# Half of x by crossbar DMA, query norms on GpSimd, two VectorE shifts in one instruction, in a gated mix of attention and MLP

## The chip, the cores and the metric

The kernel runs on one core of a Trainium2 chip. The metric is the device time of one execution in microseconds, as the median of several executions. A profiled execution has a span as well, which is 1.7 to 2.1 us shorter than its time; where stretches of one execution are compared, they are stretches of spans. The granted clock is the share of full speed at which TensorE's clock was let run; it is given where it differs.

## The reference, cut to what matters

```python
# x [1, 2048, 512]; wqkv [512, 1536]; wo [512, 512]; w_gate, w_up [512, 1792]; w_down [1792, 512]; gate_w [512]
g = sigmoid((x * gate_w).sum(-1, keepdims=True))
q, k, v = split(x @ wqkv)                      # 32 heads of 16
p = softmax(q @ k.T * 16 ** -0.5)              # 32 x 2048 x 2048 scores
a = (p @ v) @ wo
b = (sigmoid(x @ w_gate) * (x @ w_up)) @ w_down
out = g * a + (1 - g) * b                      # all in bfloat16
```

The scores are the bulk: 2048 blocks of 128 keys by 512 queries, each of which has to go through an exponential.

## The kernel before: the parts that matter

The work is cut into 32 units of 512 queries by 4 heads, 64 score blocks each. A block's exponential is taken in one of two ways. ScalarE takes two or three blocks in one Exp instruction. VectorE takes one block with an integer trick: a linear function of the score, written as a 16-bit integer whose bits are then read as a float16 (`make_x`), and two shifted copies of a pair of blocks (three phases that are averaged by three products P.V in place of one). The table `D_HALVES` says how many pairs of blocks ("halves") of each unit go to VectorE:

```python
D_PAIR = ((2, 0), (3, 1))
D_HALVES = (8, 8, 8, 8, 9, 6, 10, 8, ...)          # 32 entries, sum 267
...
def make_exp(ts):                                   # two or three blocks, ScalarE
    ... a.activation(some(PA, out), some(ps_all, bs), ACTF.Exp, bias=ACT_BIAS, scale=SCALE)
def make_x(ds):                                     # one block, VectorE
    ... v.tensor_scalar(PDu[:, bp.slot, 0, i:i + len(ds), :], some(ps_all, bs), EXP_A, EXP_B, op0=ALU.mult, op1=ALU.add)
...
for m in range(1, NPH):                             # two shifts per half
    x = P.add("dve", 0.36, lambda v, bp=bp, m=m: v.tensor_scalar(
        PDu[:, bp.slot, m, :, :], PDu[:, bp.slot, 0, :, :], float(PH_OFF[m]), None, op0=ALU.add), ...)
```

Nothing is issued in this textual order. The program holds a list scheduler: each instruction is added as a task with a planned duration, a simulation of the five engines picks an order by priorities (some forty tuned constants, many with a value per unit), and that order is then written out as five fixed instruction streams with semaphores. So the order on every engine is static, and the planned durations decide it. DMA is planned so, with one lane for all transfers:

```python
if t.dma:
    begin = max(self.dma_free, now + 2.5)
    self.dma_free = begin + t.nbytes / 330e3
    vis = self.dma_free + 0.6
```

x is loaded in plain layout and turned by TensorE, with copies out of PSUM (the memory that TensorE's products go to, `ps_all` in the lines) on VectorE and ScalarE. A query's norm is a square on GpSimd, a product with a constant matrix on TensorE and an addition on VectorE. Attention outputs are turned by DMA from SBUF to SBUF, and the MLP's output weights (`w_down`, 1.75 MB) are loaded in the middle of the run, near 158 us.

## Time and profile before

| | value |
|---|---|
| time, median of 3 (range) | 755.96 us (755.88 to 756.47) |
| profiled span, granted clock | 754.4 us, 0.999 |
| first exp starts, last exp ends | 19.9, 743.1 us |
| ScalarE idle between those two | 0.9 us |
| blocks on ScalarE, on VectorE | 1514, 534 |

The lines themselves are in the prediction below. They are read in the order busy shares, chain of waits, groups, stretches.

For the comparison I use one more measure, which needs no further lines: the length of a unit from its first exp to the first exp of the next unit. The exps run in a fixed order, and the scheduler is plain Python, so its order names the units of each exp and the trace gives the exp's start. An exp can hold blocks of two units, so one boundary can be read up to one exp (0.9 us) either way.

### The profile page before, as it was taken

The page shows a single profiled execution, that of the slowest core. Times are in us where ns is not written, and L with a number is a line of the kernel's source. Part 1 is how long each engine was busy: PE and PEld are TensorE (multiplying, and loading weights), DVE is VectorE, ACT ScalarE, POOL GpSimd, SP SyncE. Part 2 cuts the span into 40 slices and gives each one's busy share as a digit, 9 for nine tenths or more (in the row PEclk, how much of TensorE's full clock was granted, in tenths as well). Part 3 has the DMA queues.
Part 4 walks back from the last instruction along what each step waited for, and adds up shares of the span by engine and source line. Part 5 has one row for each costly group of instructions (what it writes and reads, how often), then busy time and mean ns, then how long its engine had stood idle before and what let it go on. Part 6 is the DMA issues. An engine that isn't in the chain of part 4 may idle for free.

```text
span 754.4 us, 21827 instructions
## 1 busy us (share of the span) xinstructions
PE 739.0 (98%) x9617; PEld 218.0 (29%) x9617; DVE 663.1 (88%) x1311; ACT 734.7 (97%) x822; POOL 111.4 (15%) x198
## 2 busy tenths in 40 slices
PE   8999999999999999999999999999999999999997
PEld 5233232332222222222222222222222222222222
DVE  4999999999898988778899888998889888978986
ACT  5999999999999999999999999999999999999994
POOL 4532625420100101001010010101001000000000
PEclk9999999999999999999999999999999999999999
DMA  9300000040000000000010000000000010000000
GB/s 299 121 10 9 16 4 16 9 115 9 8 9 9 16 16 22 23 2 16 9 17 9 9 23 17 22 9 17 9 1 16 16 23 23 9 10 8 15 2 30
DMA packets 34839, 19.22 MB, mean 25 GB/s; under 512 B 26688, under 2 KB 32696, under 8 KB 34744
## 3 DMA queue, kind: packets, MB, share of 16 engines
q1 hardware_dynamic: 33352, 16.38, 8.4%
q8 instruction: 75, 1.23, 0.7%
q10 hardware_dynamic: 1392, 1.44, 0.6%
q14 instruction: 20, 0.16, 0.1%
HBM read 9.70 MB, written 2.10 MB: 16 GB/s over the span
## 4 chain that ended last, share of the span: by engine, by line
ACT 75%; PE 19%; DVE 4%; DMA 1%; ACTq 0%; issue 0%; DVEq 0%
ACT PA L920 72%; PE ps_all L746 7%; PE ps_all L946 6%; PE ps_all L955 5%; ACT tT L904 3%; DVE PD L928 1%; DVE PD L984 1%; DMA PD<-in_A_x_dram 1%; PE ps_all L749 1%; PE ps_all L866 0%; DVE un L779 0%; DVE am L792 0%; PE ps_all L729 0%; DVE ost L1077 0%; ACTq L635 0%; DVE Q L830 0%
## 5 line engine op out<-in xcount | busy, mean ns | idle before, releaser
L920 ACT ACTIVATE PA<-ps_all 128x1024 bf16<-128x1024 f32 (+1 forms) x744 | 710.5, 1177 | 0.9 <-PE ps_all L946 0.5
L928 DVE TENSOR_SCALAR PD<-ps_all 128x512 uint16<-128x512 f32 x534 | 357.2, 685 | 59.8 <-PE ps_all L946 43.4
L946 PE MATMUL ps_all<-Q,K 32*128 32x512 bf16 x2048 | 301.5, 384 | 6.1 <-ACT PA L920 4.6
L955 PE MATMUL ps_all<-PA,V 128*17 128x512 bf16 x1514 | 242.3, 382 | 1.0 <-ACT PA L920 0.7
L984 DVE TENSOR_SCALAR PD<-PD 128x1024 uint16<-128x1024 uint16 x534 | 216.9, 438 | 4.2
L955 PE MATMUL ps_all<-PD,Vm 128*17 128x512 f16 x1068 | 189.9, 381 | 0.2 <-DVE PD L984 0.2
L946 PEld LDWEIGHTS ps_all<-Q,K 32*128 32x128 bf16 x2048 | 75.0, 91 | 303.5 <-ACT PA L920 272.5
L955 PE MATMUL ps_all<-PD,V 128*17 128x512 f16 x534 | 146.3, 382 | 0.0
L746 PE MATMUL ps_all<-xT,wg 128*32 128x512 bf16 x896 | 74.5, 384 | 0.0
L955 PEld LDWEIGHTS ps_all<-PA,V 128*17 128x17 bf16 x1514 | 55.9, 88 | 55.5 <-issue 43.2
L746 PE MATMUL ps_all<-un,hT 128*32 128x512 bf16 x896 | 71.7, 383 | 0.0
L746 PE MATMUL ps_all<-xT,wu 128*32 128x512 bf16 x896 | 70.0, 383 | 0.1
L1022 POOL TENSOR_TENSOR rs<-rec,e 128x16 f32<-128x16 f32 x32 | 8.3, 259 | 407.3 <-DVE rec L1020 407.3
L955 PEld LDWEIGHTS ps_all<-PD,Vm 128*17 128x17 bf16 x1068 | 44.2, 88 | 34.3 <-issue 26.2
L907 DVE SCALAR_TENSOR_TENSOR hT<-tT,ps_all 128x512 bf16<-128x512 bf16 x56 | 38.1, 680 | 8.6 <-PE ps_all L746 7.6
L904 ACT ACTIVATE tT<-ps_all 128x512 bf16<-128x512 f32 x56 | 42.7, 762 | 0.0
L831 POOL TENSOR_TENSOR qsq<-Q 128x512 bf16<-128x512 bf16 x15 | 16.0, 1069 | 159.7 <-DVE Q L830 159.7
L955 PEld LDWEIGHTS ps_all<-PD,V 128*17 128x17 bf16 x534 | 33.6, 88 | 18.5 <-issue 14.9
L784 POOL TENSOR_SCALAR K<-un,msk 128x512 bf16<-128x512 bf16 x28 | 26.6, 954 | 8.6 <-DVE un L771 5.8
L746 PEld LDWEIGHTS ps_all<-xT,wu 128*32 128x32 bf16 x896 | 19.7, 95 | 26.2 <-issue 13.6
L746 PEld LDWEIGHTS ps_all<-xT,wg 128*32 128x32 bf16 x896 | 17.8, 94 | 26.1 <-issue 20.4
L746 PEld LDWEIGHTS ps_all<-un,hT 128*32 128x32 bf16 x896 | 17.6, 94 | 24.3 <-issue 19.0
(92 smaller groups left out, 331.6 us busy)
## 6 DMA issues: line engine op xcount, KB each, us to landing
wg<-in_B_w_gate_dram SPq DMA_DIRECT2D x1, 1792.0 KB, 11.0
wu<-in_B_w_up_dram SPq DMA_DIRECT2D x1, 1792.0 KB, 14.4
un<-in_B_w_down_dram SPq DMA_DIRECT2D x1, 1792.0 KB, 8.2
out_dram<-ost SPq DMA_DIRECT2D x14, 128.0 KB, 1.8
PD<-in_A_x_dram SPq DMA_DIRECT2D x4, 256.0 KB, 5.6
PD<-in_A_x_dram ACTq DMA_DIRECT2D x4, 256.0 KB, 6.8
un<-in_A_wqkv_dram SPq DMA_DIRECT2D x2, 384.0 KB, 8.8
mid<-mid SPq DMA_TRANSPOSE x45, 2.4
```

Of the source, the lines that this page charges most:

```text
L746: i = pe.matmul(bk(b)[32 * j:32 * j + 32, :], w()[:, 32 * j:32 * j + 32], x(), start=first, stop=last, tile_position=(0, 32 * j), skip_gro ...
L749: return (MM, lambda pe: pe.matmul(bk(b), w(), x(), start=first, stop=last), four)
L784: eK[g, r, c] = P.add("pool", 1.0, lambda p, r=r: p.tensor_scalar(K[:, g, r, c * 512:(c + 1) * 512], kraw[:, kr.slot, :], msk[:, r:r + 1], ...
L831: s = P.add("pool", 1.15, lambda p: p.tensor_tensor(qsq[:, sq.slot, :], Q[:, bq.slot, 0, :], Q[:, bq.slot, 0, :], ALU.mult), [ev], [sq, bq ...
L904: et = P.add("act", 0.48, lambda a: a.activation(tT[:, t_.slot, :], bk(b), ACTF.Tanh, scale=0.5), [l1], [b, t_], kind="m")
L907: e_h[c, ft] = P.add("dve", 0.62, lambda v: v.scalar_tensor_tensor(hT[:, h_.slot, :], tT[:, t_.slot, :], 1.0, bk(b2), ALU.add, ALU.mult), ...
L920: e = P.add("act", 0.175 + 0.3665 * len(ts), lambda a: a.activation(some(PA, out), some(ps_all, bs), ACTF.Exp, bias=ACT_BIAS, scale=SCALE) ...
L928: return P.add("dve", 0.076 + 0.534 * len(ds), lambda v: v.tensor_scalar(PDu[:, bp.slot, 0, i:i + len(ds), :], some(ps_all, bs), EXP_A, EX ...
L946: return pe.matmul(bk(b), K[32 * j:32 * j + 32, g, r, kt * 128:(kt + 1) * 128], Q[32 * j:32 * j + 32, bq.slot, r, :], start=True, stop=Tru ...
L955: return pe.matmul(bk(bpv)[32 * j:32 * j + DH + 1, :], lhs(h), rhs(), start=t.first, stop=t.last, tile_position=(0, 32 * j), skip_group_ch ...
L984: x = P.add("dve", 0.36, lambda v, bp=bp, m=m: v.tensor_scalar(PDu[:, bp.slot, m, :, :], PDu[:, bp.slot, 0, :, :], float(PH_OFF[m]), None, ...
L1022: e2_ = P.add("pool", 0.2, lambda p: p.tensor_tensor(r4(rs), r4(rec), e2[:, 4 * c:4 * c + 4][:, :, None].to_broadcast([128, 4, 4]), ALU.mu ...
```

## The change

The intent: move more exponentials off ScalarE (16 more halves), and pay for it by taking other work off VectorE and TensorE: query norms by DMA and GpSimd, two shifts in one instruction, half of x turned (transposed) by the DMA crossbar on the way in. The rest is a new tuning of the scheduler. Its core, abridged, with `...` for what is cut:

```diff
-D_PAIR = ((2, 0), (3, 1))
-D_HALVES = (8, 8, 8, 8, 9, 6, 10, ...)      # sum 267
+D_PAIR = ((3, 2), (1, 0))
+D_HALVES = (9, 9, 8, 8, 10, 6, 10, ...)     # sum 283
+X_TURN, X_LOAD = (0, 1), (2, 3)
-FIN, FIN_STEP, LAST, LAST_STEP = (12.0, 18.53, 25.2), ...
+FIN, FIN_STEP, LAST, LAST_STEP = (12.33, 18.53, 24.22), ...
 ...                                          # all other constants retuned
@@ scheduler
-            begin = max(self.dma_free, now + 2.5)
-            self.dma_free = begin + t.nbytes / 330e3
-            vis = self.dma_free + 0.6
+            q = t.kind == "turn"
+            self.dma_free[q] = max(self.dma_free[q], now + (2.0 if q else 2.5)) + t.nbytes / (200e3 if q else 330e3)
+            vis = self.dma_free[q] + 0.6
 ...                                          # two ready shifts are merged; products of the next unit may go first
@@ x
+        if c in X_TURN:
+            eT[c] = [dma_t(lambda c=c: xT[:, :, 512 * c:512 * c + 512], lambda c=c: x_v[512 * c:512 * c + 512, :], ..., 524288, 60 - c, 2.1)]
@@ query norms
-    s = P.add("pool", 1.15, ... qsq = Q * Q)
-    l2 = P.group(key - 8.0, [full(b2, wn, qsq, True, True)], ...)          # TensorE
-    en = P.add("dve", 0.68, ... nsb = b2 + a_[:, g:g + 1])
+    s, d, e, _ = head_sums(lambda: Q[:, bq.slot, 0, :], [ev], [bq])        # DMA turn, GpSimd square, four halving sums
+    d2 = dma_t(lambda: mdt(s2), lambda: md(s), [e], [s, s2])
+    en = pl(0.95, ... md(s2) * -0.5 + a2[:, g:g + 1])
@@ shifts
+    def phase(x):
+        def emit(v):
+            at = sorted(b.slot for b in x.sets)                            # one or two halves
+            a = PDu[:, at[0]:at[-1] + 1:..., :, :, :]
+            return v.tensor_scalar(a[:, :, x.n, :], a[:, :, 0, :], float(PH_OFF[x.n]), None, op0=ALU.add)
-    N_PD = 3, N_MID = 11
+    N_PD = 4, N_MID = 10
 ...                                          # DMA semaphores shared, waits on the own engine kept
```

## The prediction

> **What bounds the kernel now.** I read the busy shares first, then the tenths, then the chain of waits, then the groups by form, and last three stretches of time.
>
> ```profile
> PE 739.0 (98%) x9617; PEld 218.0 (29%) x9617; DVE 663.1 (88%) x1311; ACT 734.7 (97%) x822; POOL 111.4 (15%) x198
> ACT 75%; PE 19%; DVE 4%; DMA 1%; ACTq 0%; issue 0%; DVEq 0%
> ```
>
> Three engines look full. The chain that ended last is ScalarE for three quarters; the rest is TensorE at the two ends of the span. Its pieces in order of time show what ScalarE's work costs when it follows itself:
>
> ```profile
> 2.28 7.03 DMA PD<-in_A_x_dram
> 19.98 2.31 ACT PA L920 x2
> 180.08 8.25 ACT PA L920 x9
> 188.33 0.49 ACT tT L904
> ```
>
> Nine exps over two score blocks each take 8.25 us, so 0.917 us each and 0.458 us a block (the 1164 ns below is one instruction from end to end; neighbours overlap). A tanh of the MLP takes 0.49. The groups by form:
>
> ```profile
> L920 ACT ACTIVATE PA<-ps_all 128x1024 bf16<-128x1024 f32 x718 | 677.9, 1164 | 0.5 <-PE ps_all L946 0.5
> L928 DVE TENSOR_SCALAR PD<-ps_all 128x512 uint16<-128x512 f32 x534 | 357.2, 685 | 59.8 <-PE ps_all L946 43.4 <-PE ps_all L955 13.5
> L984 DVE TENSOR_SCALAR PD<-PD 128x1024 uint16<-128x1024 uint16 x534 | 216.9, 438 | 4.2
> L920 ACT ACTIVATE PA<-ps_all 128x1536 bf16<-128x1536 f32 x26 | 39.2, 1518 | 0.4 <-PE ps_all L955 0.4
> L837 DVE TENSOR_SCALAR nsb<-ps_all,a_ 128x512 bf16<-128x512 f32 x15 | 10.9, 730 | 0.0
> L734 ACT ACTIVATE xT<-ps_all 128x1024 bf16<-128x1024 bf16 x4 | 4.1, 1024 | 3.3 <-PE ps_all L729 3.3
> ```
>
> ScalarE idles about 1 us before 744 exps. It turns 718 x 2 + 26 x 3 = 1514 of the 2048 score blocks into exps; VectorE does the other 534 by its integer trick (one read of PSUM each, and two shifts per pair of blocks). The sum closes: first exp at 19.9 us, 1514 x 0.458 = 693.4, 56 tanhs x 0.49 = 27.4, some 1.7 of small work and gaps, last exp ended at 743.1, then a tail of 11.3 to 754.4. So the middle is bound by ScalarE, to within a microsecond. VectorE and ScalarE by stretch:
>
> ```profile
> 20.00:60.00 40.00, 38.32 (x537) 12.15 (x536) 36.94 (x74) 39.80 (x44) 16.38 (x25) 1.00 0.14 50
> 60.00:150.00 90.00, 88.83 (x1343) 28.07 (x1338) 88.79 (x174) 90.00 (x98) 41.49 (x58) 1.00 0.05 11
> 300.00:500.00 200.00, 197.41 (x2437) 53.80 (x2429) 175.73 (x348) 200.00 (x227) 13.91 (x24) 1.00 0.07 15
> ```
>
> (PE, PEld, DVE, ACT, POOL in that order.) VectorE is full too until 150 us, and has 12% free from 300 to 500. TensorE's 98% is no measure, as its 384 ns records overlap. The chain shows 0.216 us a streamed matmul of 512 columns (ten in 2.16 us). In the last 20 us, where TensorE sets the pace, a set of scores with its switch into that mode takes 0.32 and two sets of others 0.55, so a switch either way costs about 0.11. My estimate of the work: some 735 score sets and 779 sets of four P.V products at 0.216; 960 full matmuls at 0.216 or their equal (projections, MLP, output, norms); and 735 x 2 x 0.11 for switches. That is 159 + 168 + 207 + 162 = 696 us in 735: TensorE has about 5% of slack. All three are near the edge, ScalarE is over it.
>
> **What the Trainium skill says.** "ScalarE: Activation LUTs", section "What ACT_TABLE_LOAD costs", gives an ACTIVATE 186 ns (280 with a pointer bias) plus 0.833 ns a column, back-to-back ones overlapping by about 93 ns. The trace has 1164 ns at 1024 columns but starts 917 apart, so an overlap of 247; I use the trace. "VectorE: DVE Perf Modes", section on the TRN2 errata, gives an SBUF to SBUF instruction 58 cycles plus a quarter of its columns in 4x mode: 325 ns for 1024 columns, 594 for 2048. The trace's closest pairs of shifts start 330 ns apart, which agrees; the fused size is not in this trace. "SBUF — State Buffer", section "Who interferes with whom", says that such VectorE instructions and GpSimd's exclude each other for a whole instruction. The trace agrees in direction. These are the shifts alone, busy time and count in the same stretches:
>
> ```profile
> 60.00:150.00 90.00, 30.41 (x68) 1.00 0.05 11
> 500.00:740.00 240.00, 69.43 (x177) 1.00 0.06 12
> ```
>
> 0.447 us where GpSimd is busy 46%, 0.392 where 5%. "DMA: Bandwidth & Descriptors", section "Latency and other measured facts", gives a crossbar transpose 261 GB/s with a non-contiguous middle dimension. This trace, in slices of 1 us from 440 on:
>
> ```profile
> DMA  6000000000000003070000000000000003000052
> GB/s 131 0 0 0 0 0 16 0 0 0 0 0 0 0 8 131 8 147 1 0 0 0 0 0 0 0 0 0 16 0 0 0 0 131 0 0 0 0 102 46
> ```
>
> The 128 KB stores (slices 16 and 34) took 0.3 of the engines' microsecond, the 128 KB transposes (slices 1 and 18) 0.6 to 0.7: about twice the DMA time a byte, near 200 GB/s. I use that.
>
> **The change, part by part.**
>
> 1. Blocks moved. The table of halves per unit sums to 283 instead of 267, so 566 blocks go to VectorE and 1482 to ScalarE. ScalarE loses 32 x 0.458 = 14.7 us on the binding path. VectorE gains 32 x 0.669 = 21.4 for the reads and 32 x 0.406 = 13.0 for the shifts (busy time over count in the groups above). TensorE gains two products per block, 64 or 16 sets of four, 3.5 us.
>
> 2. Query norms. Fifteen 0.73 us additions leave VectorE, -10.9 us, and fifteen matmuls TensorE, -3.2, with their PSUM banks. They become two transposes, a square, four halving sums and one scale-and-add per query. From the 1.05 us square and the 0.95 us masked copy in the trace I put GpSimd's extra at about 2.6 us a query, 40 in all: 111 to about 150 us. The latency of a query's norm grows from 6 us (43.5 to 50.2 for the first) to perhaps 13. Queries have four buffers and are made units ahead, so this is hidden. The cost is the lock: 0.055 us more per shift at 41 points more GpSimd, some 3.8 us per 37 us, so +4 us of VectorE for 40 more.
>
> 3. Fused shifts. Each fused pair saves one fixed cost, 0.06 us by the page and up to 0.09 by the trace's mean over its bare columns. At most 283 pairs exist; both must be ready together, which a full VectorE and a fourth buffer favour. I assume 150, -11 us. VectorE in all: 663.1 + 21.4 + 13.0 - 10.9 + 4 - 11 - 1.4 (two key copies moved to ScalarE) = 678, of a shorter span 92%. In the crowded stretch to 150 us it gets only three more halves (units 0, 1 and 4) and loses four or five norm additions: about level at 98%.
>
> 4. Start. Now x lands at 9.3, its last transpose is evacuated at 14.0, and the first exp follows 5.9 us later. Half of the 64 transposes (about 2.5 us of TensorE) and four 1.02 us ScalarE copies go. The DMA side gets dearer: 1 MB turned at 200 GB/s takes 5.2 us instead of the 3.1 at the plain rate. The last turned chunk would land near 11 to 11.5, but it is then usable at once. 11.5 + 5.9 gives 17.4; I take the first exp at 17.4, -2.5 us. ScalarE's two extra key copies (0.6 each) lie in idle time there.
>
> 5. Retuned order, a look into the next unit's products, waits on the own engine, shared DMA semaphores. I see no term of their own; they decide whether ScalarE stays fed.
>
> TensorE in all: 696 + 3.5 - 3.2 - 2.5, less 16 score sets and their switches (16 x 0.43 = 6.9): 687 of about 720. Its slack stays near 4 to 5%.
>
> Sum: span 754.4 - 14.7 - 2.5 = 737.2, plus new gaps in ScalarE that I guess at 2 us from three nearly full engines: 739.2. Timed runs lie 1.6 above the profiled span (755.96 against 754.4), so 740.8; the retuned tail may give a little back, so I say **740**.
>
> **The rivals.** (a) VectorE takes over as the bound: if few shifts fuse and the lock costs twice my figure, VectorE reaches 693 us and stays full to 150 us, and exps wait for banks there. For it: 98.7% from 60 to 150. Against: 12% free later, where most of the new halves lie. It gives 745 to 750. (b) TensorE becomes the bound, since products triple for each moved block; gaps of 5 to 8 us appear before exps. Against: the norms and score sets leave. It gives 744 to 748. (c) The crossbar feeds the start late: if turning 1 MB beside loads runs at half of 200 GB/s, the start gains nothing, 743. (d) The start gains 4 to 5 us, as evacuation and not landing set it, and the other timings leave ScalarE without gaps: 734 to 737.
>
> **Range and chances.** The 14.7 us are nearly certain, as they are counted; alone they are 1.94%. The 2% mark is 740.8 us, so the verdict hangs on the start's gain against new gaps. Range 732 to 747. Faster by over 2%: 0.55, as several freedoms (fusing, one more buffer, retuning) all point one way. Within 2%: 0.43. Slower: 0.02.
>
> **What would show it right or wrong.** Right: exps over 1482 blocks at 0.458 us, ScalarE still without idle, first exp near 17.4, VectorE near 678 with a group of 128x2048 shifts near 0.6 us, GpSimd near 150. Wrong: ScalarE idle of over 6 us released by TensorE's scores (b) or by VectorE (a); shifts over 0.5 us per 1024 columns (a); first exp after 19.5 (c); or a price per block other than 0.458, which would break the sum itself.

## The result, and the profile after

| | before | after |
|---|---|---|
| median (range) of 4 runs each, us | 755.92 (755.84 to 756.47) | 758.0 (756.42 to 759.62) |
| profiled span, us | 754.4 | 756.1 |
| first exp starts, us | 19.9 | 22.15 |
| ScalarE idle from first to last exp, us | 0.9 | 12.6 |
| ScalarE's work there, us | 722.3 | 709.2 |

The ratio is 1.0026 (95% interval 1.0004 to 1.0048): the same. Ratios here are the mean time of one kernel's fast runs over that of the other's in the same rounds, so not quite the ratio of the medians beside them. ScalarE lost 13.1 us of work and gained 11.7 of idle.

The page of the changed kernel: busy time by engine, the granted clock in 40 slices, and the chain.

```profile
PE 733.9 (97%) x9605; PEld 217.9 (29%) x9609; DVE 671.5 (89%) x1255; ACT 719.0 (95%) x793; POOL 152.6 (20%) x274
...
PEclk9999999998999999999999999999999999999999
...
ACT 68%; PE 27%; DVE 2%; DMA 1%; SPq 1%; issue 0%
```

TensorE's part of the chain rose from 19 to 27%, and one slice, the tenth (170 to 189 us), has a clock below full speed, where the kernel before had none. The groups by form:

```profile
L963 ACT ACTIVATE PA<-ps_all 128x1024 bf16<-128x1024 f32 x666 | 636.8, 1169 | 6.0 <-PE ps_all L997 5.1 <-PE ps_all L1006 0.5
L979 DVE TENSOR_SCALAR PD<-ps_all 128x512 uint16<-128x512 f32 x566 | 378.6, 685 | 50.1 <-PE ps_all L997 42.3 <-PE ps_all L1006 4.5
...
L974 DVE TENSOR_SCALAR PD<-PD 128x1024 uint16<-128x1024 uint16 x364 | 156.5, 450 | 2.2
...
L963 ACT ACTIVATE PA<-ps_all 128x1536 bf16<-128x1536 f32 x50 | 77.6, 1552 | 6.4 <-PE ps_all L997 4.6 <-PE ps_all L1006 1.7
...
L974 DVE TENSOR_SCALAR PD<-PD 128x2048 uint16<-128x2048 uint16 x101 | 71.4, 720 | 0.0
```

The operations cost in sum what they should: 666 x 2 + 50 x 3 = 1482 blocks, VectorE 671.5 us where 678 was predicted, GpSimd 152.6 where about 150 was. What is new stands in the last column: exps now wait 12.4 us, and 9.7 of that is for TensorE's scores (L997).

The two halves of x. This is the timeline of the changed kernel (start, duration, engine, line, operation; in brackets the idle time before it and what ended that):

```profile
0.79 8.24 SPq L673 DMA_TRANSPOSE xT<-in_A_x_dram  x2
...
12.40 0.22 PE L764 MATMUL ps_all<-ident,PD 128*128 128x128 bf16 x1 [1.94 <-DMA PD<-in_A_x_dram]
...
13.32 0.17 PE L891 MATMUL ps_all<-ident,gw 4*128 4x4 bf16 x1 [0.71 <-DMA gw<-in_gate_w_dram]
...
22.15 1.45 ACT L963 ACTIVATE PA<-ps_all 128x1536 bf16<-128x1536 f32 x1 [0.18 <-PE ps_all L997]
```

Two transposes of 512 KB hold their issuing queue for 8.24 us (planned: 2.1 each), the small gate weights come behind them, the last plain piece of x is used at 12.4 where the last one landed at 9.3 before, and the first exp follows 8.8 us after the gate weights.

This one profile understates how loose the new start is. Ten profiles have the changed kernel's order up to the first exp; in them it came at 20.9 to 23.7 us. In the four profiles of the kernel before and its variants it came at 19.9 to 20.0. In six of the ten the granted clock fell to half for 3.4 us between 10 and 20 us, and the first exp then came 10.2 to 10.5 us after the gate weights and not 8.8. In three it fell so between 55 and 65 us, and unit 1 took 24.8 to 25.1 us and not 23.6. So differences of 1 or 2 us in the first exp of single profiles prove little.

Where the time went, by unit lengths; differences are taken before rounding. The fifth column is what the prediction's terms give: 0.917 us per half moved, and its 2.5 us at the start.

| stretch | before, us | after, us | difference | by the prediction's terms | off by |
|---|---|---|---|---|---|
| start to first exp | 19.9 | 22.15 | +2.2 | -2.5 | 4.7 |
| units 0 and 1 | 44.5 | 45.9 | +1.4 | -1.8 (2 halves) | 3.2 |
| units 2 and 3 | 43.5 | 45.4 | +1.9 | 0 | 1.9 |
| units 4 and 5 | 45.3 | 44.1 | -1.1 | -0.9 (1 half) | -0.2 |
| units 6 to 31 | 588.9 | 585.3 | -3.6 | -11.9 (13 halves) | 8.3 |
| from the last exp's start | 12.3 | 13.2 | +1.0 | 0 | 1.0 |

The last column sums to 18.8; the prediction had allowed 2 of it as "new gaps". What makes the tail 1.0 longer was not looked into. Two places in units 6 to 31 stand out, one near 170 us and one near 300 us. The first, in the chain of waits of the changed kernel (start, duration, what):

```profile
161.97 6.21 DMA mid<-mid
...
168.21 0.25 DVE rec L1071
...
168.75 0.60 DVE hT L950
...
169.39 0.60 PE ps_all L997
170.00 0.54 PE ps_all L1006 x4
```

A 128 KB transpose of an attention output took 6.2 us to land, VectorE stood before a reciprocal of it, so the MLP product behind it in VectorE's fixed order, which frees what TensorE's next scores need, came late, TensorE waited 2.1 us, and from 170.0 on four products take 0.54 us where four at 156 took 0.22. The DMA queue of SyncE around it:

```profile
159.05 0.39 SPq L669 DMA_DIRECT2D un<-in_B_w_down_dram  x1
161.97 8.75 SPq L673 DMA_TRANSPOSE mid<-mid  x3
```

and in the kernel before:

```profile
157.77 1.18 SPq L635 DMA_DIRECT2D un<-in_B_w_down_dram  x1
162.30 1.21 SPq L639 DMA_TRANSPOSE mid<-mid  x1
```

Both kernels load w_down about 3 to 4.5 us ahead of a transpose. In the changed one three transposes follow in one row, the attention output first and one of the new query norms second, and VectorE stands before a reciprocal that waits for the first. In the kernel before, the transpose for the reciprocal stands ahead of the load in the queue. The one behind the load feeds only output products that the plan has 97 us later; it took 5.1 us to land as well, where 2.4 is the median of its 45, and nothing waited for it. So the meeting of the two transfers is old; what is new is that a short wait hangs on it. By stretch of 5 us (PE, PEld, DVE, ACT, POOL busy, then clock, DMA share, GB/s):

```profile
165.00:170.00 5.00, 2.90 (x36) 0.69 (x31) 2.00 (x6) 3.58 (x4) 1.27 (x3) 0.93 0.83 110
170.00:175.00 5.00, 5.00 (x40) 0.95 (x43) 3.36 (x6) 2.59 (x4) 0.32 (x1) 0.50 0.14 30
175.00:180.00 5.00, 5.00 (x58) 1.09 (x51) 4.06 (x8) 4.34 (x5) 0.00 (x0) 0.89 0.01 3
```

ScalarE idles 1.42 + 2.41 + 0.66 = 4.5 us here, most of it not during the wait but after it, at half the clock.

Near 300 us nothing waits for DMA. Unit 12 just takes 26.2 us after and 23.0 before, with 50 blocks on ScalarE in both. TensorE's groups in unit 12, first before, then after:

```profile
L746 PE MATMUL ps_all<-un,hT 128*32 128x512 bf16 x96 | 7.9, 383 | 0.0
...
L746 PE MATMUL ps_all<-wo,mid 128*32 128x512 bf16 x16 | 1.4, 382 | 0.0
```

```profile
L778 PE MATMUL ps_all<-un,hT 128*32 128x512 bf16 x140 | 9.9, 382 | 0.0
...
L778 PE MATMUL ps_all<-wo,mid 128*32 128x512 bf16 x48 | 4.2, 381 | 0.0
```

These are the output products of the first 512 tokens, four of them side by side at a time: 188 where there were 112. The constant FIN, moved from 12.0 to 12.33, places them. The 76 more are 19 sets of four, 4.1 us at the prediction's 0.216 a set.

### The profile page after: what moved, and what is told of

Read it like the earlier page. It is cut to its first block, busy times and chain, and to the rows that moved or that the text cites. A ratio compares the mean times of both kernels' runs of the same rounds, so it can differ in the third digit from the quotient of the medians.

```text
span 756.1 us, 21810 instructions
## 1 busy us (share of the span) xinstructions
PE 733.9 (97%) x9605; PEld 217.9 (29%) x9609; DVE 671.5 (89%) x1255; ACT 719.0 (95%) x793; POOL 152.6 (20%) x274
## 3 DMA queue, kind: packets, MB, share of 16 engines
q1 hardware_dynamic: 53320, 20.32, 12.3%
## 4 chain that ended last, share of the span: by engine, by line
ACT 68%; PE 27%; DVE 2%; DMA 1%; SPq 1%; issue 0%
ACT PA L963 65%; PE ps_all L997 10%; PE ps_all L778 8%; PE ps_all L1006 7%; ACT tT L947 3%; PE ps_all L906 1%; SPq L673 1%; DVE PD L979 1%; DMA mid<-mid 1%; PE ps_all L781 1%; DMA gw<-in_gate_w_dram 1%; PE ps_all L909 0%; DVE PD L974 0%; DVE V L922 0%; DVE un L824 0%
## 5 line engine op out<-in xcount | busy, mean ns | idle before, releaser
L963 ACT ACTIVATE PA<-ps_all 128x1024 bf16<-128x1024 f32 (+1 forms) x716 | 697.0, 1196 | 12.4 <-PE ps_all L997 9.7
L979 DVE TENSOR_SCALAR PD<-ps_all 128x512 uint16<-128x512 f32 x566 | 378.6, 685 | 50.1 <-PE ps_all L997 42.3
L997 PE MATMUL ps_all<-Q,K 32*128 32x512 bf16 x2048 | 301.7, 385 | 10.5 <-ACT PA L963 6.1
L1006 PE MATMUL ps_all<-PA,V 128*17 128x512 bf16 x1482 | 237.9, 383 | 0.6 <-ACT PA L963 0.3
L974 DVE TENSOR_SCALAR PD<-PD 128x1024 uint16<-128x1024 uint16 (+1 forms) x465 | 226.2, 508 | 2.2
L1006 PE MATMUL ps_all<-PD,Vm 128*17 128x512 f16 x1132 | 199.1, 383 | 0.0
L997 PEld LDWEIGHTS ps_all<-Q,K 32*128 32x128 bf16 x2048 | 75.4, 91 | 298.7 <-ACT PA L963 253.8
L1006 PE MATMUL ps_all<-PD,V 128*17 128x512 f16 x566 | 150.5, 383 | 0.0
L778 PE MATMUL ps_all<-un,hT 128*32 128x512 bf16 x896 | 69.3, 382 | 0.0
L1006 PEld LDWEIGHTS ps_all<-PD,V 128*17 128x17 bf16 x566 | 34.0, 88 | 17.0 <-issue 12.4
L797 POOL TENSOR_TENSOR mid<-mid 128x256 bf16<-128x256 bf16 (+3 forms) x60 | 30.1, 501 | 4.4
L878 POOL COPY Q<-Q 128x512 bf16<-128x512 bf16 x15 | 11.0, 735 | 95.4 <-DVE Q L877 95.4
L778 PEld LDWEIGHTS ps_all<-xT,wu 128*32 128x32 bf16 x896 | 19.4, 95 | 25.9 <-issue 10.6
L1053 DVE CAST mid<-ps_all 128x512 bf16<-128x512 f32 x32 | 21.8, 682 | 5.1 <-PE ps_all L1006 5.1
```

Of the source, the lines that this page charges most:

```text
L778: i = pe.matmul(bk(b)[32 * j:32 * j + 32, :], w()[:, 32 * j:32 * j + 32], x(), start=first, stop=last, tile_position=(0, 32 * j), skip_gro ...
L797: e = pl(0.22 + 0.054 * n, lambda g, n=n: g.tensor_tensor(v()[:, :, 0:n], v()[:, :, 0:n], v()[:, :, n:2 * n], ALU.add), [e], prio=0.5, buf ...
L878: cp = P.add("pool", 0.7, lambda p: p.tensor_copy(Q[:, bq.slot, 1, :], Q[:, bq.slot, 0, :]), [ev], [bq], kind="m")
L963: e = P.add("act", 0.175 + 0.3665 * len(ts), lambda a: a.activation(some(PA, out), some(ps_all, bs), ACTF.Exp, bias=ACT_BIAS, scale=SCALE) ...
L974: return v.tensor_scalar(a[:, :, x.n, :], a[:, :, 0, :], float(PH_OFF[x.n]), None, op0=ALU.add)
L979: return P.add("dve", 0.076 + 0.534 * len(ds), lambda v: v.tensor_scalar(PDu[:, bp.slot, 0, i:i + len(ds), :], some(ps_all, bs), EXP_A, EX ...
```

## The experiments

Theory at this point (**the load**): the expected gain went into ScalarE's new idle time, and the largest single piece comes from w_down meeting a transpose. Rivals: **the start** (queue order and crossbar), **VectorE or GpSimd** as the new bound (lock, unfused shifts), **a wrong price** per block, and **TensorE** as the bound. Twelve runs test the pieces; six more, the last section of these, test the premise. All times are medians; the median of the kernel before stood at 755.9 to 756.4 us beside each. Where an edit moves one DMA in its queue, it is made after planning, so every other order stays as it was.

### Gate weights first

```diff
+    sp.remove(egw); sp.insert(0, egw)        # load gate_w ahead of the two transposes
```

> The changed kernel with every engine's order kept, but the 1 KB load of gate_w issued ahead of the two crossbar transposes in SyncE's queue. In the changed kernel it was issued at 9.1 us, landed at 13.3, and TensorE stood before its tiny transpose with the last key projections behind it. Theory A (the time is lost at a few places where transfers queue behind transfers): first exp from 22.15 to about 21.2, time 0.5 to 1 us shorter. Theory B (TensorE and VectorE are full, so ScalarE starves whenever they set the pace): the first exp is earlier but the time changes by less than 0.5 us.

Measured: 759.61 us, ratio 1.0045 (1.0031 to 1.0058). The wait for the gate weights is gone, but the transposes behind them came later: TensorE stood 5.56 us before the turned x, until 11.67, and ran at half the clock for 3.4 us after it; the first exp was at 24.2. So the edit gained nothing, but it moved the wait from one transfer of the queue to another, and doesn't clear the queue of blame for the start. The stall near 170 us stayed (clock 0.69 in 170 to 175).

### w_down on another queue

```diff
+    P.order["sp"].remove(e_wd); e_wd.eng = "act"; act.insert(..., e_wd)
```

> The changed kernel with every engine's order kept, but the 1.75 MB load of w_down issued from ScalarE's queue instead of SyncE's, where three transposes stood behind it (6.2 us in the chain that ended last, then TensorE's clock at half for 5 us). Theory A: the 4.5 us that ScalarE idles from 165 to 180 us and the dip of the clock go, time 3 to 5 us shorter (753 to 755). Theory B: the idle comes back at a later place, time within 1 us of the changed kernel.

Measured: 756.97 us, 1.0016 (1.0003 to 1.0028). The load went out on ScalarE's queue at 157.8 us and the transpose still took 6.35 us to land; ScalarE idled 4.1 us in 165 to 175 and the clock fell to 0.53. So SyncE's queue is not what is short. What the two transfers still share are the 16 DMA engines.

### x by plain load in the crossbar's place (wrong result)

```diff
+            eT[c][0].emit = lambda e, c=c: e.dma_start(xT[:, :, 512 * c:512 * c + 512], x_p[:, 4 * c:4 * c + 4, :])
```

> Wrong result on purpose: the two crossbar transposes of x become plain loads of the same bytes into the same buffer; all else and every order is kept. Theory A (the transposes hold up the start): x lands near 9.5 instead of 12.4, the first exp comes at 18 to 19 instead of 22.15, time 3 to 4 us shorter. Theory B: the early stage to 60 us is bound by VectorE and TensorE, so ScalarE's idle there grows by most of what the start gains; time at most 1 us shorter.

Measured: 756.85 us, 1.0009 (0.9995 to 1.0022). x is there by 11 us and the first exp at 19.98 (20.07 in the other run with plain loads): 2.2 us before the changed kernel's profile, 0.8 to 3.8 before those of the ten. But only about 1 us reaches the end, no more than the noise of these runs. Unit 1 here takes 25.1 us in place of 23.6 (granted clock 0.93 from 45 to 68 us) and gives most of it back.

### Old table of halves in the changed kernel

```diff
-D_HALVES = (9, 9, 8, 8, 10, 6, 10, ...)
+D_HALVES = (8, 8, 8, 8, 9, 6, 10, ...)
```

> The changed kernel with the table of halves of the kernel before (534 blocks on VectorE, 1514 on ScalarE); the order is planned anew, with settings that were tuned for the other table. If ScalarE is the bound and each block costs it 0.458 us, this is 13 to 15 us longer than the changed kernel (771 to 773), less what other engines give back. If the other engines are the bound (theory B), it is within 4 us of the changed kernel or faster.

Measured: 769.91 us, 1.0189 (1.0165 to 1.0212), so 12 us over the changed kernel for 32 blocks put back on ScalarE (14.7 by the price). The direction and size fit the price, but the constants are tuned to the new table and the scheduler planned a new order, in which ScalarE idles 11.6 us as well. It speaks against the halves being worth nothing; it doesn't measure their price exactly.

### w_down later

```diff
+    sp.remove(e_wd)
+    i = next(i for i, t in enumerate(sp) if t.start > 170.0)    # behind the transposes of 162 us
+    sp.insert(i, e_wd)
```

> The changed kernel with every engine's order kept, but w_down's 1.75 MB load placed later in SyncE's queue, after the query loads of 170 us, where the trace shows 20 us without a transpose. Moving it to another queue did nothing, as the transpose of the attention output still took 6.3 us to land beside it, and VectorE's reciprocal, TensorE behind it and then the clock waited. Theory A (transfers that meet in the DMA engines): ScalarE's 4.5 us of idle from 165 to 180 us and the clock of 0.5 go, time 3.5 to 5 us shorter than the changed kernel (753 to 754.5). Theory B (engines full, ScalarE starves anyway): the idle comes back elsewhere, within 1.5 us of the changed kernel.

Measured: 753.25 us, 0.9962 (0.9950 to 0.9974): 4.75 us under the changed kernel, and under the kernel before by 0.4%. The same stretches, the first two:

```profile
165.00:170.00 5.00, 5.00 (x69) 1.33 (x65) 4.72 (x9) 5.00 (x7) 1.61 (x3) 1.00 0.27 54
170.00:175.00 5.00, 5.00 (x65) 1.36 (x61) 4.76 (x10) 5.00 (x7) 0.00 (x0) 1.00 0.90 291
```

ScalarE is full, the clock is 1.00, and the load runs at 291 GB/s in the second stretch without harm, because no transpose is waited for there. Units 6 to 31 fall from 585.3 to 580.2 us. This settles the first of the two places: one transfer, 4.5 us of idle, 4.75 us of time.

### Both of these

```diff
+            eT[c][0].emit = ...              # as in the plain load above: wrong result
+    sp.insert(i, e_wd)                       # as above
```

> Wrong result on purpose: the late w_down load and plain loads in place of the two crossbar transposes of x, together, order kept. Theory A: first exp at 20.0, no idle from 165 to 180, the two gains add to 5 or 6 us: 751.5 to 753. What then remains (5 us of idle to 90 us, 3 near 300) was in the plan. Theory B: not below 755.

Measured: 751.75 us, 0.9938 (0.9924 to 0.9953). The first exp came at 20.07, 1.0 us before that of the late load's own profile (21.11), and the median is 1.5 us lower. As far as the intervals tell, the two effects add.

### Shifts one by one

```diff
-            return v.tensor_scalar(a[:, :, x.n, :], a[:, :, 0, :], float(PH_OFF[x.n]), None, op0=ALU.add)
+            for s in at:
+                r = v.tensor_scalar(PDu[:, s, x.n, :, :], PDu[:, s, 0, :, :], float(PH_OFF[x.n]), None, op0=ALU.add)
+            return r
```

> The changed kernel, order kept, each of the 101 fused shifts of 2048 columns issued as two of 1024. VectorE's shifts take 0.43 us bare and 0.707 fused in the changed kernel, so VectorE gains 15 us of work. If VectorE had slack everywhere (ScalarE the bound) the time grows by under 2 us; if VectorE sets the pace in the stretches where ScalarE starves, it grows by 4 to 12 us.

Measured: 763.18 us (758.37 to 767.75), 1.0093 (1.0060 to 1.0127). The same shifts take 236.1 us of VectorE in place of 226.2 and the median is 5 us higher. The saving is 0.10 us a fused pair, 9.9 us in all where 15 was expected. What it is worth in time is not shown: the four times go roughly with their clocks (758.37 us at 0.998, 763.90 at 0.992, 762.46 at 0.990, 767.75 at 0.984), and the profile, of the slowest, has a clock of 0.81 from 130 to 165 us. VectorE did set the pace from 110 to 127 us there.

### Less GpSimd work (wrong by construction, inside the tolerance)

```diff
-        e = pl(1.07, lambda g: g.tensor_tensor(md(s), md(s), md(s), ALU.mult), ...)
+        e = pl(1.07, lambda g: g.tensor_tensor(md(s)[:, 0:16], md(s)[:, 0:16], md(s)[:, 0:16], ALU.mult), ...)
 ...                                          # the halving sums and the scale likewise
```

> Wrong result on purpose: the square, the halving sums and the scale of the query norms on GpSimd run on 16 or 32 columns instead of 512 to 1024, order and count kept. GpSimd's busy time falls by about 30 us. If the lock between GpSimd and VectorE's shifts matters, bare shifts fall from 0.43 to 0.40 us, VectorE loses 8 to 12 us of busy time, ScalarE's idle to 90 us shrinks by 1 to 3 us and the time by as much. If it does not matter, the time stays within 1 us.

Measured: 757.79 us, 1.0022 (1.0009 to 1.0035), no change. GpSimd fell from 152.6 to 118.8 us, single shifts from 450 to 439 ns, fused ones from 720 to 693, VectorE by 5 us in all. So GpSimd's work does lengthen the shifts, by about the size predicted, and no cost in time shows.

### Fewer columns for the output products of the first quarter (wrong result)

```diff
-        mms, deps, bufs = final_mms(c, st, b, range(NFT), range(4), True)
+        mms, deps, bufs = final_mms(c, st, b, range(NFT), range(4), True, 128 if c == 0 else 512)
```

with the late w_down.

> Wrong result on purpose, on top of the late w_down load (753.25 us): the four output products of the first query chunk, which TensorE runs near 290 to 310 us, move 128 columns instead of 512; order kept. ScalarE idles 3.05 us there. If TensorE sets the pace there, that idle goes and the time falls by 2.5 to 3.5 us. If VectorE or a transfer does, the idle stays and the time changes by under 1 us.

Measured: 756.88 us, 1.0003 (0.9975 to 1.0032), 3.6 us slower than the same kernel with the full products. The stretch around unit 12:

```profile
290.00:310.00 20.00, 16.46 (x274) 6.17 (x274) 12.59 (x26) 15.89 (x15) 0.84 (x2) 0.83 0.12 28
```

TensorE has less to do, 16.46 busy for 19.95 with the full products, and a clock of 0.83 for 1.00; unit 12 took 27.7 us for 26.1. The test is spoiled by the clock and says nothing on the question it was made for.

### Less VectorE work in units 1 to 3

```diff
+            PDu[:, bp.slot, 0, i:i + len(ds), 0:512 - LIGHT * (0 < ds[0].unit < 4)], some(ps_all, bs)[:, :, 0:512 - ...], EXP_A, EXP_B, ...
```

with `LIGHT = 256` and the late w_down (wrong by construction).

> Wrong result on purpose, on top of the late w_down load: VectorE's reads of scores in units 1 to 3 (26 blocks, about 47 to 111 us) cover 256 of the 512 columns, 0.27 us less each, 7 us of VectorE in all; order kept. ScalarE idles 4.0 us from 50 to 90 us there. If VectorE sets the pace there, the idle falls by 2 us or more and the time too. If TensorE does, the idle stays within 1 us.

Measured: 752.73 us, 0.9955 (0.9940 to 0.9970), 0.5 us under the late w_down alone; ScalarE's idle from 50 to 90 us fell from 4.0 to 2.3 us, a little less than the mark of 2, and units 2 and 3 from 45.4 to 44.8 us. VectorE alone isn't the pace of these units.

### A scheduler with one DMA lane

```diff
-            self.dma_free[q] = max(self.dma_free[q], ...) + t.nbytes / (200e3 if q else 330e3)
+            self.dma_free[0] = max(self.dma_free[0], ...) + t.nbytes / (200e3 if q else 330e3)
-  ..., 524288, 60 - c, 2.1)
+  ..., 524288, 60 - c, 4.1)                  # the queue is held 4.1 us per 512 KB
 ...                                          # constants retuned by a local search under this model, 281 halves
```

> The changed kernel with its scheduler corrected in two places that the traces showed wrong (all transfers share one lane of DMA time, and a crossbar transpose of 512 KB holds SyncE's queue 4.1 us instead of 2.1), and the knobs searched anew for the corrected plan; 281 halves, all parts of the change kept. The plan now ends at 743.0; the kernel before's plan ended at 750.7 and ran in 754.4, 3.7 later. If the loss was in transfers that the plan did not see (theory A), the span is within 6 us of the plan and the time 747 to 751, faster than both kernels. If VectorE and TensorE starve ScalarE however the transfers are planned (theory B), it does not get below 753.

Measured: 753.06 us, 0.9955 (0.9943 to 0.9967). Theory A missed both of its marks: the span of 750.8 is 7.8 us behind the plan, and the time above 751; it stands on the edge of theory B's 753. The stall near 170 us is gone, and the kernel is as good as with the hand-moved load, though its start was bad: the first exp came at 24.6 us, planned 19.5. The corrected model and the new search came together, so what the model alone does isn't shown.

### One lane, and no crossbar for x

```diff
-X_TURN, X_LOAD = (0, 1), (2, 3)
+X_TURN, X_LOAD = (), (0, 1, 2, 3)            # all of x by plain loads and TensorE, 284 halves, retuned
```

> The same correction and search, but all of x by plain loads and TensorE transposes as in the kernel before; 284 halves. Plan: end at 746.9. Tells whether the crossbar part of the change is worth anything once planned for: expected 750 to 754, 2 to 4 us longer than its sister with the crossbar; first exp near 19.5 against 21 there.

Measured: 751.42 us, 0.9940 (0.9927 to 0.9953), with a right result: the fastest valid version, 0.6% under the kernel before. It was 1.6 us faster than its sister with the crossbar, where 2 to 4 us slower was expected; its first exp came at 19.7. Norms by DMA and GpSimd, fused shifts and 17 more halves are all in it; the crossbar for x is not. ScalarE still idles about 10 us.

### Six runs on the premise: who sets the pace?

By now about 8 us of the 18.8 were open (units 0 to 5, and unit 12), and what remained in doubt was the premise itself. These runs take ScalarE's work away where it is said to be the bound, and leave every order as it is. An exp that covers 256 columns per block in place of 512 takes about 0.5 us for two blocks in place of 0.92; the results are wrong by construction. One look each, with clocks of 0.997 to 0.999.

```diff
+    def part(t):
+        return 256 if t.unit in LIGHT else 512
-  a.activation(some(PA, out), some(ps_all, bs), ACTF.Exp, ...)
+  a.activation(some(PA, out)[:, :, 0:part(ts[0])], some(ps_all, bs)[:, :, 0:part(ts[0])], ACTF.Exp, ...)
```

First with `LIGHT = (2, 3, 12, 20)` in the changed kernel with the late w_down:

> Wrong result on purpose. The changed kernel with the late w_down load; in units 2, 3, 12 and 20 every exp covers half of its columns, order unchanged, so ScalarE needs about 0.5 us an exp in place of 0.92 there and cannot be what paces these units. Without the edit (from first exp to first exp): units 2 and 3 together 45.3 us, unit 12 26.5, unit 20 21.2; in the kernel before, with the same halves on VectorE, the first two take 44.1 and 22.9. Theory T (TensorE's work in its fixed order is longer than ScalarE's in units 2, 3 and 12, and ScalarE waits for it): 2 and 3 stay at 43.5 or more, unit 12 at 25.5 or more, and only unit 20 falls, to about 20. Theory S (ScalarE paces these units too, and the idle time comes from how the two wait for each other): 2 and 3 fall under 41, unit 12 under 23. Theory V (VectorE paces them): as T here, but not in the next run.

then the same for VectorE's reads of scores as well:

> Wrong result on purpose. As the run before, and VectorE's reads of scores cover half of their columns as well in the same units, so only TensorE keeps its full work there. Theory T: the same lengths as in the run before to within 0.5 us. Theory V: units 2 and 3 fall by 2 us or more against the run before.

and the exps alone in the kernel before:

> Wrong result on purpose. The kernel before with the same halving of exps in its units 2, 3, 12 and 20 (44.1, 22.9 and 21.5 us unedited). It shows what TensorE alone takes there in the order of the kernel before. If the new order put more TensorE work into unit 12 than the old one (theory T), unit 12 falls here to 22 or less while it stays at 25.5 or more in the changed kernel; units 2 and 3 to about 42 to 43. Under S all fall about as far as in the changed kernel.

Measured, in us (first exp to first exp):

| | units 2 and 3 | unit 12 | unit 20 | span |
|---|---|---|---|---|
| changed, late w_down | 45.4 | 26.1 | 20.2 | 751.5 |
| exps halved | 43.9 | 25.3 | 19.4 | 748.1 |
| exps and VectorE's reads halved | 42.1 | 25.1 | 19.4 | 747.1 |
| before | 43.5 | 23.0 | 21.5 | 754.4 |
| before, exps halved | 43.1 | 22.9 | 21.0 | 753.5 |

My theory T held for unit 12 of the changed kernel, which hardly moved (25.3 is just under the mark of 25.5, which came from the rougher count). For units 2 and 3 it held against ScalarE alone, not in the second run. And I had the wrong idea of the kernel before: I expected its unit 12 at 22 or less and its units 2 and 3 at 42 to 43, and neither moved by more than 0.4. Taking some 30 us of ScalarE's work out of four units brought that kernel 0.9 us. With the exps halved, units 2 and 3 of the changed kernel look so:

```profile
69.00:114.00 45.00, 44.58 (x747) 15.10 (x734) 44.97 (x83) 29.39 (x49) 24.91 (x40) 1.00 0.12 20
```

ScalarE is busy 29.39 us of 45.00, VectorE 44.97: VectorE is the pace once ScalarE is out of the way (its own relief then brings 1.8 us, somewhat under the 2 I had named as the mark for it), and TensorE comes next with 42.1. Unit 12 of the changed kernel needs 25.1 us with both relieved, against 22.9 in the kernel before: this is what its 76 extra products cost, and no exp can be faster than its scores.

Then over the whole middle, units 6 to 31, in both kernels:

> Wrong result on purpose. The kernel before, with every exp of units 6 to 31 over half of its columns, order unchanged; this takes about 40% of ScalarE's work out of these units. They take 588.9 us unedited (first exp of unit 6 to the last exp). If ScalarE alone bounds the kernel before and TensorE has the 4 to 5% of slack of the prediction, they fall to about 560. If TensorE and VectorE, in their fixed order, are as long as ScalarE, which the last three runs make me expect, they stay at 580 or more.

> Wrong result on purpose. The same, and VectorE's reads of scores over half of their columns in these units, so that TensorE alone keeps its work. Slack of 5% in TensorE: about 560. If TensorE's order is as long as ScalarE's: 575 or more. If it falls by 10 us or more against the run before, VectorE had paced that one.

> Wrong result on purpose. The changed kernel with the late w_down load, exps and VectorE's reads halved in units 6 to 31, which take 579.9 us unedited. From the units measured alone (20.4 for 21.2, 25.6 for 26.5) I expect about 560, a slack of 3.5%; under the theory that TensorE's order is what the new kernel waits for throughout, 572 or more.

| first exp of unit 6 to the last exp's start, us | all work | exps halved | exps and VectorE's reads halved |
|---|---|---|---|
| before | 588.9 | 581.2 | 574.7 |
| changed, late w_down | 580.2 | not run | 562.1 |

The lines for 200 to 700 us, of the kernel before:

```profile
200.00:700.00 500.00, 494.41 (x6153) 136.03 (x6151) 438.73 (x864) 499.73 (x561) 35.12 (x62) 1.00 0.06 14
```

of the kernel before with the exps halved:

```profile
200.00:700.00 500.00, 498.41 (x6235) 137.46 (x6228) 442.88 (x879) 336.06 (x569) 35.24 (x63) 1.00 0.06 14
```

and of the changed kernel with both halved:

```profile
200.00:700.00 500.00, 499.65 (x6456) 138.83 (x6452) 378.31 (x881) 338.91 (x568) 61.84 (x111) 1.00 0.10 19
```

In the first line ScalarE looks like the only bound, with 499.73 us of 500. In the second it works 336 us, a third less, and in 500 us only 1.3% more products are done (6235 for 6153). So in the kernel before, TensorE and VectorE in their fixed orders were 7.7 us behind ScalarE in units 6 to 31, 1.3%. TensorE nearly by itself (VectorE keeps its shifts, but is busy 366 us of 500) was 14.2 us behind, 2.4%, about half of the 4 to 5% of the prediction. In the changed kernel its slack there is 18.1 us, 3.1% (562.1 of 580.2): the change did shorten TensorE's order, by 12.5 us, and there the moved blocks did pay.

## Why the prediction was wrong, point by point

- **The price per block was right.** 1482 blocks instead of 1514, and ScalarE's work fell by 13.1 us where 14.7 was the sum. The sums for VectorE (671.5 for 678), for GpSimd (152.6 for 150) and the hidden latency of the norms held too. Only 101 shifts were fused of the 150 assumed. A fused shift is followed by VectorE's next instruction after 0.599 us in the median, as the 0.594 worked out from the page says; from end to end it takes 0.72, and the page says under that table that its formula is too short for a single instruction (0.693 us measured for 2048 columns). The extra GpSimd work cost no time when it was tested. Three slips in the prediction's sums change nothing: ScalarE's small work and gaps are 2.4 us and not 1.7, the page's formula gives 327 ns for 1024 columns and not 325, and the profiled run before took 756.18, so 1.8 above its span and not 1.6.
- **The step that failed is the "new gaps in ScalarE that I guess at 2 us".** They were 11.7. Some 4.5 us of it is the DMA stall near 170 us, for which the sum had no term. The rest failed because it rested on "So the middle is bound by ScalarE, to within a microsecond" and on "Its slack stays near 4 to 5%". ScalarE was busy to within a microsecond, which isn't the same as being the only bound. The runs show the next bound 1.3% behind in units 6 to 31 of the kernel before, and 0.4 us of 43.5 in units 2 and 3. Of the prediction's own signs of being wrong two came true: over 6 us of idle released by TensorE's scores, and a first exp after 19.5. So "nearly certain, as they are counted" was wrong of the 14.7: they come only where the other engines' orders get shorter too, stretch by stretch.
- **Units 6 to 31 (8.3 of the 18.8).** Without the w_down stall they fall by 8.7 of the expected 11.9; the 3.2 that are missing are what unit 12 grew by, 3.1. So here the term was sound, less two things: 5.1 us for one DMA that the plan, with its own lane for crossbar transfers, thought free, shown by moving the load; and some 3 us for TensorE's extra products in unit 12, shown by the 25.1 us that it needs there with the other two engines relieved. Neither was visible in the profile before. The first was visible in the diff, as the second lane.
- **The start (4.7) and units 0 to 5 (4.9).** The start term was -2.5 and came out as +2.2. I had put the last turned chunk at 11 to 11.5 and 5.9 us from there to the first exp. The last piece was used at 12.4, the gate weights at 13.3, and it took 8.8 us from those at full clock, with or without the crossbar, and up to 10.5 where the clock fell. Rival (c) had the direction, with too small a size. The plain load shows that the crossbar accounts for about 2 us of the first exp, give or take the 1.5 by which profiles differ, and about 1 us of the time. In units 2 and 3 rival (a) was half right, as VectorE and TensorE set the pace there; that the same holds in units 0 and 1 is argued from VectorE's full stretches, and not tested. Unit 0 took 22.3 us in both kernels; unit 1 is the one that grew, from 22.2 to 23.6, and what exactly holds it stays open. Units 4 and 5 gained what was expected.
- **Rival (b)**, TensorE becoming the bound with exps waiting for scores, came nearest in mechanism. It gave 744 to 748, as it knew of no stall and kept the gain at the start.
- **The scheduler knew part of it.** Its own simulation of the two kernels ends at 750.7 and 744.3 us, so it promised 6.3 us and not 15, and had 18 us of ScalarE idle time planned, 7 of it between 20 and 80 us. A plan in the source is worth running, which takes no chip: where the constants moved that place work, units may have got more than they can hold.
- **Also unforeseen:** the changed kernel's runs spread over 3.2 us, the kernel before's over 0.6. The drops of the clock in the start and in unit 1, which come in some profiles and not in others, are a likely cause; the runs don't prove it, as each has one profile.

## What to carry to other kernels

An engine without idle time is not the only bound: before pricing what its relief brings, ask stretch by stretch how long the other engines' fixed orders would take without it, and where a chip is at hand, halve that engine's work without changing the order and look how little moves. In a statically ordered kernel a single late transfer can be paid twice, as here, once as the wait and once as the slower clock after it, so keep big loads away from small transfers that an in-order engine waits for, and let the planner's model of DMA be one shared resource.

## What the Trainium skill lacked or had wrong

- "TensorE: Matmul & The Clock Gate", section "HAM oscillation — how this bites in real kernels", names TensorE gaps of over about 3.4 us as the danger; its next section, "A second HAM failure mode: psum-queue depth-cycling", says that frequent short idles can do it too, without a size. Here a stretch of 5 us in which TensorE was busy 2.90 us, with 2.10 us as its last wait, was enough for a clock of 0.50 over the next 5 us; and taking work out of a stretch, so that TensorE was busy 16.46 us of 20 with no gap over 0.7 us, gave a clock of 0.83 there.
- "DMA: Bandwidth & Descriptors", section "Latency and other measured facts", gives a rate for transposes, and no page says what a transpose loses beside a large load: a 128 KB transpose between SBUF buffers that met a 1.75 MB load took 6.2 us to land, and 6.35 with the load on another queue, where the median in the kernel before is 2.4. Nor does the section say how long a transpose from HBM holds the queue that issues it: 8.24 us for two of 512 KB.
- No page that I read says that a busy share of nearly 100% may hide an equal bound on another engine: ScalarE's 499.73 us of 500 became 336, and units 6 to 31 were 1.3% shorter.
